# Ten chunks of a two-stage layer keep their rows in stored order, with additions moved to GpSimd and copies to other queues

## The chip, the cores and the metric

The kernel runs on one core of a Trainium2 chip. A core has engines that run side by side: TensorE (PE; its weight loads are shown as PEld), VectorE (DVE), ScalarE (ACT), GpSimd (POOL) and SyncE (SP), and 16 DMA engines that they share. The metric is the device time of one execution in microseconds; the median of several runs is given.

## The reference

Two layers follow each other. The first is a linear attention with a feature map of exponentials over 8 batches, 8 heads, 576 tokens and 64 channels; its output, put together over the heads, is `x` with shape (8, 576, 512). The second mixes `x` over the tokens in the frequency domain, with a 512 by 512 complex matrix for each of 64 modes, and closes with a channel product:

```python
X = np.fft.rfft(x, axis=1)
Y = np.zeros_like(X)
Xr, Xi = (np.real(X[:, :n_modes]), np.imag(X[:, :n_modes]))
Yr = np.einsum('bmd,mde->bme', Xr, w_r) - np.einsum('bmd,mde->bme', Xi, w_i)
Yi = np.einsum('bmd,mde->bme', Xr, w_i) + np.einsum('bmd,mde->bme', Xi, w_r)
Y[:, :n_modes] = Yr + 1j * Yi
y = np.fft.irfft(Y, n=S, axis=1)
u = x + y
return (u + np.maximum(u @ w_ch, 0.0)).astype(np.float32)
```

The mode weights `w_r` and `w_i` are 64 x 512 x 512 each and are most of what is read.

## The kernel before

The first 298 us work through 16 units of attention (four channel groups `g` by four batch pairs `bp`). They leave `x` in SBUF as bf16 (`xs`) and its spectrum (`XT`). Meanwhile the mode weights come in by loads of 1024 KB on GpSimd's DMA queue (`wload`, `next_w`); each goes to a slot of the pool `pw` (tag `wt`, eight slots). `mix` multiplies one load with the spectrum; when it has finished, the next load may take the slot.

From 298 us on, work on `x` is placed between the mixes. `x` is cut into 36 chunks `(bp, n)` of 128 rows and 512 columns, nine for each batch pair. Three stages follow.

- **Hold** (`hold`, class `Channels`). A chunk is transposed by TensorE, VectorE copies the transpose to `xT`, TensorE multiplies it with the channel weights `wchb`, and ScalarE copies the product to `xw`. The last three chunks keep their product in PSUM.
- **Absorb** (class `Absorb`). The modes are done in eight groups `o` of eight. When the first six groups are mixed, their inverse transform is added to each chunk: TensorE multiplies the table `CI` (96 rows) with `yall` (sums of the modes) and `zall` (the sums times the channel weights). VectorE adds the first to `xs`, and ScalarE writes the second, summed with the old `xw`, back to `xw`.
- **Last** (class `Last`, and the loop over `seq` at the end). When the last two groups are mixed, each pair of chunks is closed. In `base`, TensorE multiplies `xw` (result `q`) and `xs` (result `p`) with the permutation `perm`, which brings rows into stored order; the chunks of n = 8 use the identity, as their rows are in order already. In `late` it adds the last two groups through the table `CL` and the copies in `yl`. ScalarE takes the Relu of `q` into the tile `rl`, VectorE adds `p` and `rl` into an output tile `of` (slots of `pw`, tag `wt`; two of the eight hold `yall` and `yl`), and SyncE starts the store.

`put` spreads the sums: for `o` below 6 one DMA writes 16 rows of `yall` or `zall`; for `o` of 6 and 7 the sums are copied to two places each in `yl`, so that products of a pair can use different rows of TensorE at one time.

The order within each engine is the order written in the program (`InOrder` keeps it). The list `todo` holds the steps of hold and absorb, and `fill` runs some after each mix; how many is worked out from `A`, the number of steps left for the last seven mixes. `bank` gives one of four PSUM banks, `banks` one of two double banks. In `seq`, the Relu side of a pair is made one step ahead of its closing addition.

Of the kernel before, what the change touches and what calls it, by code (L numbers as in the profile page):

```python
# [19 lines left out]
DMODEL = 512  # L20
# [23 lines left out]
def kernel(  # L44
# [533 lines left out]
    CI = pb.tile([128, 5, 128], BF16, name="CI", bufs=1)  # L578
    CL = pb.tile([128, 5, 128], BF16, name="CL", bufs=1)
    perm = CF.rearrange("p c t x m -> p (c t x m)")[:, 512:640]  # L580
# [5 lines left out]
    def inverse_tables():  # L586
# [37 lines left out]
        for dst, m, r, only in ((CI, mode, r, None), (CL, late, r, None), (CM, last, rm, b0)):  # L624
            n = 512 if only is not None else 640
# [13 lines left out]
            dve.tensor_tensor(out=ang[:, :n], in0=ang[:, :n], in1=rnd[:, :n], op=ALU.add)  # L639
            yield  # L640
            act.activation(rnd[:, :n], ang[:, :n], ACT.Sin, scale=2.0 * math.pi / S_)
            if dst is CI:
                dve.tensor_scalar_mul(out=dst.rearrange("p c s -> p (c s)"), in0=rnd[:, :n],
                                      scalar1=amp)
                yield
                continue
# [5 lines left out]
            if dst is CL:  # L652
                dve.tensor_scalar_mul(out=dst[:, 4, :], in0=rnd[:, 512:640], scalar1=amp)
            yield

    class Channels:
# [4 lines left out]
        def turn(self):  # L661
            x = chunk(self.bp, self.n)
            pt = bank([128, 4, 128], BF16)
            for g in range(NG):
                pe.transpose(pt[:, g, :], x[:, g, :], ident_b)
            self.xT = pb.tile([128, 4, 128], BF16, name="xT")
            dve.tensor_copy(self.xT, pt)

# [11 lines left out]

    def back(p, c, bp, table, src, r, stop=True):

        if c < 8:
            pe.matmul(p, lhsT=table[r, c % 4, :], rhs=src[r, 2 * bp + c // 4, :],
                      start=(src is yall), stop=stop)
        else:
            for i in range(2):
                pe.matmul(p[64 * i:64 * i + 64, :], lhsT=table[r, 4, 0:64],
                          rhs=src[r, 2 * bp + i, :], start=(src is yall), stop=True)

    class Absorb:

        def __init__(self, bp, n):
            self.bp, self.n = bp, n

        def sum_p(self, p):
            self.p = p
            back(p, self.n, self.bp, CI, yall, slice(0, 96))

        def sum_q(self, q):  # L700
            self.q = q
            pe.matmul(q, lhsT=ident_b, rhs=xw[:, self.bp, self.n, :], start=True, stop=False)
            back(q, self.n, self.bp, CI, zall, slice(0, 96))

# [12 lines left out]
        def only_w(self):  # L717
            back(self.q, self.n, self.bp, CI, zall, slice(0, 96))
            self.keep_w()
# [11 lines left out]

    chunks = [(bp, n) for bp in range(NP) for n in range(9)]
    ch = [Channels(*c) for c in chunks]
    ab = [Absorb(*c) for c in chunks]
# [4 lines left out]
    def hold(i):  # L739
# [3 lines left out]
        if i < K:  # L743
            ch[i].product()
            return
        if i == K:
# [6 lines left out]
    todo = [ch[0].turn] + [lambda i=i: hold(i) for i in range(len(ch))]  # L753
    todo += [c.only_x for c in ab[K:]] + [c.only_w for c in ab[K:]] + [c.all for c in ab[:K]]
    A = 3 * 3 + K

# [5 lines left out]
    def put(src, o, dst, copies):  # L762
        if o < 6:
            sp.dma_start(dst[16 * o:16 * o + 16], src)
        else:
            for s in copies:
                r = 32 * s + 16 * (o - 6)
                (sp, pool)[s // 2 if o == 7 else 0].dma_start(yl[r:r + 16], src)


    class Last:

        def __init__(self, *items):
# [24 lines left out]
        def late(self, which):  # L798
            for a, (bp, n) in enumerate(self.items):
                r = 64 * a + 32 * which  # L800
                back((self.q if which else self.p)[a], n, bp, CL, yl,
                     slice(r, r + 16 if self.early else r + 32), not self.early)

# [10 lines left out]
        def relu(self):  # L814
            self.rl = pb.tile([128, 2, DMODEL], F32, name="rl")
            for a in range(len(self.items)):
                act.activation(self.rl[:, a], self.q[a], ACT.Relu)

        def store(self):
# [10 lines left out]
            else:  # L830
                dve.tensor_tensor(out=o, in0=self.pp, in1=self.rl, op=ALU.add)
            if n == 8:
                sp.dma_start(
# [9 lines left out]
    pairs = [[((bp, n), (bp, n + 1)) for n in (0, 2, 4, 6)] for bp in range(NP)]  # L843
    seq = [Last((0, 0)), Last((0, 1))] + [Last(*x) for x in pairs[0][1:] + pairs[1]]
    seq += [Last((0, 8), (1, 8))] + [Last(*x) for x in pairs[2]] + [Last((2, 8), (3, 8))]
    seq += [Last(*x) for x in pairs[3][:3]] + [Last((3, 6)), Last((3, 7))]
    H = DMODEL // 2
    while mixq:
# [113 lines left out]
```

## Time and profile before

| | us |
|---|---|
| median of 7 runs | 445.13 |
| lowest and highest | 443.82, 445.69 |
| the profiled execution's own time | 444.2 |
| span of the profiled execution | 442.3 |
| PE busy | 341.1 |
| DVE busy | 284.6 |
| ACT busy | 279.2 |
| POOL busy | 84.5 |

The profile is of one execution. Its span leaves out what lies around the program's instructions. A line of a timeline has the start in us from the span's start, the duration, the engine, the line, the operation with its tiles, and in brackets the idle time before it with what ended that. All instructions pass through the helper on line 37, so they are told apart by their tiles. DMA share is the mean busy share of the 16 DMA engines; a share above 1 comes from transfers that overlap in an engine.

### The profile page before, as it was taken

What the parts mean: (1) busy time and instruction counts of PE and PEld (TensorE: products, weight loads), DVE (VectorE), ACT (ScalarE), POOL (GpSimd) and SP (SyncE); (2) the same over time, 40 slices, a digit from 0 to 9 for tenths busy, and PEclk for the clock granted to TensorE, in tenths of its full rate; (3) what the DMA queues carried; (4) which work ended last, traced back from release to release, by engine and by line L of the source; (5) the groups of instructions that cost most, each with busy time, mean ns of one, the idle gap of its engine ahead of it and who ended that gap; (6) DMA issues with size and microseconds to landing.
All of it is one profiled execution on the core that took longest, in us unless ns stands there. A gap on an engine that the chain in (4) does not pass through costs nothing.

```text
span 442.3 us, 10508 instructions
## 1 busy us (share of the span) xinstructions
PE 341.1 (77%) x4433; PEld 216.4 (49%) x4433; DVE 284.6 (64%) x561; ACT 279.2 (63%) x488; POOL 84.5 (19%) x126
## 2 busy tenths in 40 slices
PE   3567768777697786795886777876899859999994
PEld 2346547645575564564754655652455424343231
DVE  4667586555756766867668668759844323876685
ACT  4598687666867976966777659433444322665673
POOL 7132122121211312321222011141011110000000
PEclk9689888688978989988888889698899999999998
DMA  8999999999999999999999999999999999993697
GB/s 170 236 211 210 238 212 237 237 212 264 210 212 237 238 236 235 213 239 210 239 220 229 234 215 240 211 213 212 211 224 221 219 219 219 212 221 80 216 382 286
DMA packets 51487, 99.31 MB, mean 225 GB/s; under 512 B 2480, under 2 KB 13616, under 8 KB 51440
## 3 DMA queue, kind: packets, MB, share of 16 engines
q0 software_dynamic: 45280, 86.19, 99.2%
q1 hardware_dynamic: 6160, 12.45, 8.1%
q8 instruction: 34, 0.56, 0.5%
q14 instruction: 13, 0.11, 0.1%
HBM read 163.64 MB, written 9.44 MB: 391 GB/s over the span
## 4 chain that ended last, share of the span: by engine, by line
issue 32%; PE 26%; DMA 14%; ACT 11%; DVE 8%; POOL 8%; POOLq 0%; ACTq 0%; DVEq 0%
DMA wt<-in_moe_w_i_dram 13%; PE pt L37 8%; PE one L37 7%; PE pp L37 5%; PE two L37 5%; POOL wt L37 4%; ACT AB L37 4%; DVE m L37 3%; ACT AQ L37 2%; DVE mk L37 2%; DVE xs L37 1%; ACT XT L37 1%; POOL qb L37 1%; ACT qT L37 1%; POOL kb L37 1%
## 5 line engine op out<-in xcount | busy, mean ns | idle before, releaser
L37 ACT ACTIVATE AB<-two 128x1024 bf16<-128x1024 f32 x64 | 62.2, 1032 | 11.6 <-DVE mk L37 8.2
L37 ACT ACTIVATE AQ<-two 128x1024 bf16<-128x1024 f32 x64 | 62.8, 1049 | 3.6 <-PE two L37 3.4
L37 ACT CAST xw<-pt 128x512 bf16<-128x512 f32 x50 | 29.4, 587 | 41.1 <-PE pt L37 41.1
L37 DVE TENSOR_REDUCE mk<-two 128x8 f32<-128x1024 f32 x32 | 38.9, 1219 | 14.5 <-PE two L37 14.5
L37 DVE TENSOR_REDUCE m<-two 128x8 f32<-128x1024 f32 x32 | 39.2, 1225 | 12.5 <-PE two L37 12.4
L37 DVE RECIPROCAL rd<-one 128x6 f32<-128x6 f32 x48 | 9.4, 196 | 54.8 <-PE one L37 54.7
L37 DVE TENSOR_TENSOR va<-vn,ee 128x1152 bf16<-128x1152 f32 x32 | 42.0, 1356 | 0.0
L37 PE MATMUL pt<-wchb,xT 128*128 128x512 bf16 x136 | 37.6, 402 | 5.6 <-DVE xT L37 4.2
L37 ACT COPY kT<-one 128x512 bf16<-128x512 bf16 (+1 forms) x32 | 19.3, 640 | 30.2 <-PE one L37 30.1
L37 PEld LDWEIGHTS <-xs 128*128 128x128 bf16 x624 | 31.8, 103 | 12.8 <-issue 7.0
L37 PEld LDWEIGHTS <-minus 96*128 96x128 bf16 x288 | 28.1, 116 | 18.5 <-issue 13.3
L37 PE MATMUL two<-w2blk,qT 128*128 128x256 bf16 x128 | 20.5, 285 | 20.7 <-ACT AB L37 10.9
L37 POOL DMA_DIRECT2D wt<-in_moe_w_r_dram x30 | 22.4, 745 | 69.4 <-PE one L37 34.8
L37 POOL DMA_DIRECT2D wt<-in_moe_w_i_dram x28 | 20.9, 746 | 75.4 <-PE one L37 42.0
L37 PE MATMUL two<-qT,w2blk 128*128 128x512 bf16 x64 | 30.3, 474 | 4.4 <-ACT AQ L37 4.1
L37 PEld LDWEIGHTS <-qT 128*128 128x128 bf16 x144 | 13.9, 99 | 37.9 <-issue 35.6
L37 PE MATMUL one<-wt,XT 128*32 128x512 bf16 x304 | 27.1, 443 | 6.6 <-DVE XT L37 2.7
L37 PE MATMUL two<-mT,minus 96*128 96x128 bf16 x256 | 30.8, 255 | 0.0
L37 PE MATMUL one<-kvz,AQ 128*128 128x65 bf16 x512 | 29.6, 217 | 0.0
L37 PEld LDWEIGHTS <-XT 128*32 128x32 bf16 x512 | 14.4, 149 | 28.1 <-issue 15.8
L37 DVE TENSOR_TENSOR xs<-one,rd 128x384 bf16<-128x384 f32 x48 | 26.8, 558 | 1.7
L37 PEld LDWEIGHTS <-AQ 128*128 128x128 bf16 x512 | 26.5, 116 | 1.4 <-issue 0.4
(131 smaller groups left out, 692.0 us busy)
## 6 DMA issues: line engine op xcount, KB each, us to landing
wt<-in_moe_w_r_dram POOLq DMA_DIRECT2D x30, 1024.0 KB, 22.1
wt<-in_moe_w_i_dram POOLq DMA_DIRECT2D x28, 1024.0 KB, 22.4
vn<-in_v_dram POOLq DMA_DIRECT2D x15, 576.0 KB, 17.6
out_dram<-of SPq DMA_DIRECT2D x16, 512.0 KB, 3.0
kb<-in_k_dram POOLq DMA_DIRECT2D x16, 288.0 KB, 15.8
qb<-in_q_dram POOLq DMA_DIRECT2D x16, 288.0 KB, 16.2
xs<-in_moe_w_i_dram POOLq DMA_DIRECT2D x2, 1024.0 KB, 24.6
yacc<-in_moe_w_r_dram POOLq DMA_DIRECT2D x1, 1024.0 KB, 9.8
```

What stands on the lines that cost most here:

```text
L37: ins = f(*args, **kwargs)
```

## The change

- Ten chunks (five pairs, the list `stored`) are turned to stored order in the hold stage: the copy to `xT` interleaves the columns, and `back_x` transposes `xT` back and writes it over the chunk in `xs`. Their absorb uses a new table `CD`, which is `CI` with interleaved columns.
- In the last stage these pairs need no `perm`; `xw` is multiplied with the identity, `xs` is not multiplied at all. GpSimd adds the chunk to the Relu result, in a tile `rx` from the slots of `pw`, and VectorE adds the late part to that.
- The four chunks of n = 8 go to the front of the list and get no absorb. In the last stage they take all eight groups at once, through `CI` with 128 rows from `yall` and `zall`, which `put` now fills for `o` of 6 and 7 too (on GpSimd's queue). Their `xs` is added by GpSimd as well.
- For `o` = 6 the copies to the upper two places of `yl` move from SyncE's queue to GpSimd's; for `o` = 7 all copies to `yl` are on SyncE's.
- The closing loop has a new order. A table `ahead` says for which pair the Relu side is made at each step; pairs whose sums go through GpSimd are made two to three steps ahead. The two double chunks of n = 8 are in a table `whole`.

```diff
+    CD = pb.tile([128, 4, 128], BF16, name="CD", bufs=1)
+    stored = [(1, 0), (1, 1), (1, 4), (1, 5), (2, 0), (2, 1), (2, 6), (2, 7), (3, 4), (3, 5)]
...
+                for a in range(2):
+                    dve.tensor_copy(
+                        CD.rearrange("k c (p a) -> k a c p", a=2)[:, a],
+                        CI[:, 0:4].rearrange("k c (a p) -> k a c p", a=2)[:, a])
...
-            dve.tensor_copy(self.xT, pt)
+            if (self.bp, self.n) in stored:
+                dve.tensor_copy(self.xT.rearrange("p g (k a) -> p g a k", a=2),
+                                pt.rearrange("p g (a k) -> p g a k", a=2))
+            else:
+                dve.tensor_copy(self.xT, pt)
+
+        def back_x(self):
+            px = bank([128, 4, 128], BF16)
+            for g in range(NG):
+                pe.transpose(px[:, g, :], self.xT[:, g, :], ident_b)
+            act.copy(chunk(self.bp, self.n), px)
...
+            self.table = CD if (bp, n) in stored else CI
...
+    chunks.sort(key=lambda c: (c[1] < 8, c not in stored))
...
             ch[i].product()
+            if chunks[i] in stored:
+                ch[i].back_x()
...
-    todo += [c.only_x for c in ab[K:]] + [c.only_w for c in ab[K:]] + [c.all for c in ab[:K]]
-    A = 3 * 3 + K
+    todo += [c.only_x for c in ab[K:]] + [c.only_w for c in ab[K:]] + [c.all for c in ab[NP:K]]
+    A = 3 * 3 + K - NP
...
-        else:
-            for s in copies:
-                r = 32 * s + 16 * (o - 6)
-                (sp, pool)[s // 2 if o == 7 else 0].dma_start(yl[r:r + 16], src)
+            return
+        for s in copies:
+            r = 32 * s + 16 * (o - 6)
+            (pool if o == 6 and s > 1 else sp).dma_start(yl[r:r + 16], src)
+        pool.dma_start(dst[16 * o:16 * o + 16], src)
...
+            self.direct = n == 8
+            self.later = self.direct or items[0] in stored
...
-                turned = perm if n < 8 else ident_b
+                turned = ident_b if self.later else perm
+                if self.later and not which:
+                    continue
...
+                if self.direct:
+                    back((self.q if which else self.p)[a], n, bp, CI, zall if which else yall,
+                         slice(0, 128))
+                    continue
...
-            self.rl = pb.tile([128, 2, DMODEL], F32, name="rl")
+            if self.later:
+                self.rl = pw.tile([128, 2, DMODEL], F32, name="rx", tag="wt")
+            else:
+                self.rl = pb.tile([128, 2, DMODEL], F32, name="rl")
             for a in range(len(self.items)):
                 act.activation(self.rl[:, a], self.q[a], ACT.Relu)
+            if self.later:
+                for a, c in enumerate(self.items):
+                    x = self.rl[:, a].rearrange("p (g e) -> p g e", g=4)
+                    pool.tensor_tensor(out=x, in0=x, in1=chunk(*c), op=ALU.add)
...
+    whole = {10: Last((0, 8), (1, 8)), 13: Last((2, 8), (3, 8))}
...
+    ahead = {1: 2, 2: 3, 3: 4, 4: 7, 5: 6, 6: 9, 7: 8, 8: 10, 9: 12, 10: 11, 11: 13, 12: 15, 13: 14,
+             14: 16, 15: 17}
     for g, s in enumerate(seq):
-        t = seq[g + 1] if 0 < g < len(seq) - 1 else None
-        if t and g > 1:
+        t = seq[ahead[g]] if g in ahead else None
+        if t and g not in (1, 3):
             t.base(1)
-        if g > 1:
+        if g > 1 and g != 3:
             s.base(0)
-            if g == 2:
-                s.late(0)
-                s.straight(0)
+        if g == 2:
+            s.late(0)
+            s.straight(0)
+            seq[4].base(1)
+            seq[3].base(0)
...
         s.store()
+        extra = [whole[g + 3]] if g + 3 in whole else [seq[5]] if g == 3 else []
+        for d in extra:
+            d.base(1)
+            d.late(1)
+            d.relu()
+        if g in whole:
+            d = whole[g]
+            d.base(0)
+            d.late(0)
+            d.store()
```

The stored pairs stand at places 5, 7, 9, 12 and 15 of the new `seq`; places 16 and 17 are single chunks.

More of the change, by code (lines that the diff above doesn't have):

```diff
@@ L578 @@
     CI = pb.tile([128, 5, 128], BF16, name="CI", bufs=1)
-    CL = pb.tile([128, 5, 128], BF16, name="CL", bufs=1)
+    CL = pb.tile([128, 4, 128], BF16, name="CL", bufs=1)
+    CD = pb.tile([128, 4, 128], BF16, name="CD", bufs=1)
+    stored = [(1, 0), (1, 1), (1, 4), (1, 5), (2, 0), (2, 1), (2, 6), (2, 7), (3, 4), (3, 5)]
     perm = CF.rearrange("p c t x m -> p (c t x m)")[:, 512:640]
@@ L624, in inverse_tables @@
         for dst, m, r, only in ((CI, mode, r, None), (CL, late, r, None), (CM, last, rm, b0)):
-            n = 512 if only is not None else 640
+            n = 640 if dst is CI else 512
             ph = calc(r, -S_ / 4.0, S_ / 4.0)
@@ L645, in inverse_tables @@
                 yield
+                for a in range(2):
+                    dve.tensor_copy(
+                        CD.rearrange("k c (p a) -> k a c p", a=2)[:, a],
+                        CI[:, 0:4].rearrange("k c (a p) -> k a c p", a=2)[:, a])
+                yield
                 continue
@@ L651, in inverse_tables @@
                     scalar1=amp)
-            if dst is CL:
-                dve.tensor_scalar_mul(out=dst[:, 4, :], in0=rnd[:, 512:640], scalar1=amp)
             yield
@@ L679, in hold, with back @@
                           start=(g == 0), stop=False)
-    def back(p, c, bp, table, src, r, stop=True):
+    def back(p, c, bp, table, src, r, stop=True, start=False):
         if c < 8:
             pe.matmul(p, lhsT=table[r, c % 4, :], rhs=src[r, 2 * bp + c // 4, :],
-                      start=(src is yall), stop=stop)
+                      start=start or src is yall, stop=stop)
         else:
@@ L694, in __init__ @@
             self.bp, self.n = bp, n
+            self.table = CD if (bp, n) in stored else CI
         def sum_p(self, p):
             self.p = p
-            back(p, self.n, self.bp, CI, yall, slice(0, 96))
+            back(p, self.n, self.bp, self.table, yall, slice(0, 96))
         def sum_q(self, q):
@@ L702, in sum_q @@
             pe.matmul(q, lhsT=ident_b, rhs=xw[:, self.bp, self.n, :], start=True, stop=False)
-            back(q, self.n, self.bp, CI, zall, slice(0, 96))
+            back(q, self.n, self.bp, self.table, zall, slice(0, 96))
         def keep_x(self):
@@ L717, in only_w @@
         def only_w(self):
-            back(self.q, self.n, self.bp, CI, zall, slice(0, 96))
+            back(self.q, self.n, self.bp, self.table, zall, slice(0, 96))
             self.keep_w()
@@ L799, in late @@
             for a, (bp, n) in enumerate(self.items):
+                if self.direct:
+                    back((self.q if which else self.p)[a], n, bp, CI, zall if which else yall,
+                         slice(0, 128))
+                    continue
                 r = 64 * a + 32 * which
                 back((self.q if which else self.p)[a], n, bp, CL, yl,
-                     slice(r, r + 16 if self.early else r + 32), not self.early)
+                     slice(r, r + 16 if self.early else r + 32), not self.early,
+                     self.later and not which)
         def straight(self, which):
@@ L831, in store @@
                 dve.tensor_tensor(out=o, in0=self.pp, in1=self.rl, op=ALU.add)
-            if n == 8:
+            if self.direct:
                 sp.dma_start(
@@ L843 @@
     pairs = [[((bp, n), (bp, n + 1)) for n in (0, 2, 4, 6)] for bp in range(NP)]
-    seq = [Last((0, 0)), Last((0, 1))] + [Last(*x) for x in pairs[0][1:] + pairs[1]]
-    seq += [Last((0, 8), (1, 8))] + [Last(*x) for x in pairs[2]] + [Last((2, 8), (3, 8))]
+    seq = [Last((0, 0)), Last((0, 1))] + [Last(*x) for x in pairs[0][1:] + pairs[1] + pairs[2]]
     seq += [Last(*x) for x in pairs[3][:3]] + [Last((3, 6)), Last((3, 7))]
+    whole = {10: Last((0, 8), (1, 8)), 13: Last((2, 8), (3, 8))}
     H = DMODEL // 2
```

## The prediction

> **What bounds the kernel now.** I read the busy shares by slice first, then the windows by stage, the timeline of the last 75 us engine by engine, and the answers for single weight loads.
>
> From the page's slices (tenths of 40 slices of 11 us):
> ```profile
> span 442.3 us, 10508 instructions
> ...
> PEclk9689888688978989988888889698899999999998
> DMA  8999999999999999999999999999999999993697
> ```
> The DMA engines are full until slice 36 (398 us), nearly idle for one slice, and busy again with the output. So there is a loading part set by DMA, and a closing part after the last weights.
>
> Windows by stage (us, then busy time of PE, PEld, DVE, ACT, POOL, then clock, DMA share, GB/s):
> ```profile
> 395.00:400.00 5.00, 5.00 (x29) 1.83 (x28) 3.88 (x8) 3.22 (x6) 0.00 (x0) 1.00 1.14 192
> 400.00:405.00 5.00, 4.85 (x27) 1.67 (x24) 3.90 (x7) 3.39 (x7) 0.00 (x0) 1.00 0.37 70
> 405.00:410.00 5.00, 4.99 (x34) 2.14 (x33) 1.83 (x5) 1.74 (x4) 0.90 (x2) 1.00 0.21 52
> 420.00:425.00 5.00, 5.00 (x34) 1.62 (x31) 4.05 (x5) 3.55 (x8) 0.00 (x0) 1.00 0.95 386
> ```
> Before 405 us PE looks full (absorbs), and DMA tapers off: one of two limits, PE or the last load. The granted clock is 1.00 throughout. GpSimd is idle.
>
> The load that the last mix needs (its issue and landing):
> ```profile
> L37 POOL DMA_DIRECT2D wt<-in_moe_w_i_dram x1: 740/740/740, 369.4 to 369.4; - x1
> ...
> DMA to landing us min/median/max: 35.7/35.7/35.7
> ```
> It lands at 369.4 + 35.7 = 405.1; the last mix starts at 405.42. PE and DMA arrive together, so freeing PE alone gains 0.3 us there.
>
> VectorE in the closing part (start, duration, and in brackets the idle time before and its releaser):
> ```profile
> 412.71 1.23 DVE L37 TENSOR_TENSOR of<-pp,rl 128x1024 f32<-128x1024 f32 x1 [1.32 <-PE pp L37]
> 415.22 6.39 DVE L37 TENSOR_TENSOR of<-pp,rl 128x1024 f32<-128x1024 f32 x5 [1.28 <-PE pp L37]
> 421.94 1.23 DVE L37 TENSOR_TENSOR of<-pp,rl 128x1024 f32<-128x1024 f32 x1 [0.34 <-PE pp L37]
> 423.58 5.17 DVE L37 TENSOR_TENSOR of<-pp,rl 128x1024 f32<-128x1024 f32 x4 [0.41 <-PE pp L37]
> 429.09 1.23 DVE L37 TENSOR_TENSOR of<-pp,rl 128x1024 f32<-128x1024 f32 x1 [0.34 <-PE pp L37]
> 430.73 5.01 DVE L37 TENSOR_TENSOR of<-pp,rl 128x1024 f32<-128x1024 f32 x4 [0.41 <-PE pp L37]
> 435.66 0.68 DVE L37 TENSOR_TENSOR ofr<-pp,rl 128x512 f32<-128x512 f32 x1
> 436.58 0.69 DVE L37 TENSOR_TENSOR ofr<-pp,rl 128x512 f32<-128x512 f32 x1 [0.24 <-ACT rl L37]
> ```
> VectorE makes a pair of output rows every 6.39 / 5 = 1.28 us. A PE step takes 1.30 us (its base multiplications for successive pairs start at 424.70 and 426.00). So from 415.22 to 437.27 two engines are level, and VectorE idles only 2 x (0.34 + 0.41) = 1.50 us, at the two pairs of n = 8. The stores run at 386 GB/s with DMA share 0.95: a third limit close by.
>
> **The sum's frame.** The profiled execution took 444.2 us: 442.3 of span and 1.9 around it. The median of the seven runs is 445.13, 0.93 higher; I work on 444.2 and add 0.93 at the end. About 0.2% (0.9 us) is what a measurement of this kernel can tell from no change.
>
> **Holding stage, 298 to 372 us: cost nothing.** Ten chunks get four transposes back (0.23 us of PE each: a transpose group starts at 328.40, the next group at 328.63), a ScalarE copy (0.64, the kT copy's row) and a strided xT copy (0.42 now; a strided 128x128 copy took 0.30, so 0.7 for 512). That is 2.3 us of PE, 6.4 of ACT, 2.8 of DVE, and under 1 us for CD's two copies. What hides it is PE's idle time before weights land: 1.74 at 350.20, 0.91 at 355.53, 3.23 at 361.69, 5.9 us in all. Without that cover it would cost about 2.6 us. Weight issues come a little later, but each load now queues 32 to 38 us.
>
> **Absorb stage, 372 to 405 us.** Four n = 8 absorbs go. Three are whole, 0.99 us of PE each (390.61 to 391.60). The fourth goes in two parts of 0.33; another chunk takes its place among the last three, 0.65 becoming 0.44. Together 3.86 us, so PE could be at the last mix at 405.42 - 3.86 = 401.6, or 402.9 with the waits for earlier loads (about 1.3). An idle time of about 1 us does not slow PE: after 0.91 idle at 355.53 four products took 1.03 us, while after 3.23 idle at 361.69 eight small ones took 1.89 against 1.04.
>
> So the landing decides. The loads of 351.17, 356.50, 362.67 and 369.40 land after 35.8, 37.6, 37.4 and 35.7: at 387.0, 394.1, 400.1, 405.1. Undisturbed spacing is 5.0 (the load of 346.49 lands after 35.5, at 382.0), so three loads took 18.1 instead of 15.0. In that stretch SyncE's queue carries the four copies of the o = 6 sums (4 x 128 KB, issued 385.91 to 389). The change leaves two there; the other two, and the two new writes into yall and zall, go on GpSimd's queue, in program order behind all weight loads (last issue 369.40). Half of 3.1 is **1.55 us earlier**. Bounds: at the 220 GB/s of these windows 256 KB take 1.2; at most 2.4, where PE itself arrives (402.9 with 0.1 to start). The later landing of the two copies is free: pair (0,2) needs them at 409.97, some 5 us after the weights.
>
> At o = 7 both copies of each sum go on SyncE, one after the other (0.55 an issue), where GpSimd's copy was issued at 409.66 and PE waited for it until 413.36. Same time within 0.3 us. Behind them on SyncE is only the first store (410.37).
>
> **Closing stage, in the times of before.**
> - Removed: ten base multiplications of x (5 x 0.44 us of PE), the four n = 8 ones, and the 1.50 us of VectorE idle time that follows the n = 8 groups. VectorE still adds every pair, 15 x 1.28 + 1.5.
> - Moved: two pairs of base multiplications go ahead of the wait for yl. But pair 3's two Relus then start at 413.9 and last 1.08, so VectorE starts on it at 415.1 against 415.22. Nothing gained.
> - Added: 14 GpSimd adds of 128x512 between Relu and VectorE. No such row exists. The same add on VectorE takes 0.69; GpSimd's one-input 128x128 row took 0.292 and an empty MEMSET 0.098, so 512 elements take 0.098 + 4 x 0.194 = 0.87 with one input and up to 0.098 + 8 x 0.194 = 1.65 with two. I take **1.1**, between these; both ends stay for the range.
>
> Three more waits follow. ScalarE makes Relus in the order 3, 4, 5, 7, 6: from 413.9 five pairs at 1.09, so pair 6 is ready at 419.4. Pair 5's first half is ready at 416.7; two adds end at 418.95, and VectorE, due at 417.66, starts pair 5 at 419.0 and pair 6 at 420.3. Twelve pairs at 1.28 from there and 1.5 for the two single rows end at 437.1, against 437.27: the idle time that goes is spent at pair 5. Later adds fit while 14 of them from 416.75 end before pair 15 is due at 434.4, that is up to 1.26 each.
>
> Last, buffers. The early Relu results (rx) take the same six free slots as the output tiles. An output tile holds one 1.23 + 3.0 us (landing of a store), 3.3 slots at this pace; seven rx of about 5 us in 16 us hold 2.2. Of six slots 5.5 are full, so jitter becomes stalls; with PSUM waits at the two extra pairs I take **0.6**, between 0 and 1.6 (stores that land at 3.4, the top of the usual rows, at each reuse). Tail: -0.2 + 0.6 = **+0.4**.
>
> The Trainium skill's GPSIMD Engine Reference, section "Elementwise — side-by-side cycle accounting", speaks against this step: it gives 4497 ns for a 2048-element fp32 add on GpSimd and 2293 on VectorE. A quarter of that is an estimate of 1.12 us and a fixed part, and with 1.2 the sum would be 0.2 us later than mine. Its SBUF page ("SBUF — State Buffer", "Who interferes with whom") has VectorE and GpSimd lock a shared port pair; by its rule a VectorE add with one input in PSUM would not wait, and nothing in this trace shows either.
>
> **Sum.** 444.2 - 1.55 + 0.4 = 443.05, 1.15 less; on the median 445.13 - 1.15, **444.0 us**. Own range of this case 443.0 to 445.0.
>
> **The rivals.**
> - GpSimd becomes the bound. It decides from 1.26 us an add. At 1.4 the 14 adds end at 436.35 and the tail at 439.1, +1.9; at 1.65 at 439.85 and 442.6, +5.3. With -1.55 the kernel ends at 445.5 to 448.9. For it: two inputs, one strided and of another type. Against: it needs the upper third of my price. Chance 0.25.
> - The queue change brings nothing, because the last load is late for another reason (the taper from 400 to 405 us), or the copies only move: -0 + 0.4, 445.5. Against it: the spacing of 5.0 before 387 and 7.1 right after. Chance 0.15.
> - Both terms at their better ends: last mix when PE is ready (-2.4), adds at 0.87 or less and no slot stalls (ScalarE's order then sets pair 6 at 419.45, the tail is 1.0 shorter): 441.7. Chance 0.15.
> - My forecast: 0.45.
>
> **Chances and range.** Faster by over 0.2% (below 444.24): 0.30 of my forecast's 0.45 and the 0.15 of the better ends, 0.45. Within 0.2%: 0.15 of the forecast, 0.05 of the queue rival, 0.03 of the first, 0.23. Slower: 0.10 and 0.22, 0.32. The range 441.7 to 447.5 leaves out GpSimd's price above 1.55 (about 0.1) and gains beyond both better ends.
>
> **What would show it.** Last landing at 403.5 and last mix within 0.3 of it, PE idle about 1 us before; a GpSimd row of 14 adds at 1.1 us; VectorE idle about 1.3 us before pair 5, then pairs at 1.28 with waits on store landings. It is wrong if the adds take over 1.26 us, if the landing stays at 405, or if PE still loses time in the holding stage.

## The result: 0.4% slower, and the profile after

The changed kernel takes 446.47 us (median of 15 runs, 445.47 to 447.70) against 444.73 for the kernel before beside it (36 runs): a ratio of the means of 1.0042, 95% interval 1.0032 to 1.0051. A second set of four runs gave 447.57 and 1.0067 [1.0046, 1.0088]. The forecast was 444.0, with faster as the likeliest sign; the sign was wrong. That the time still lies inside the outer range of 441.7 to 447.5 is luck: the upper part of that range was there for GpSimd as the bound, and GpSimd was not the bound. The profiled execution took 446.47 us, 2.27 more than the one before; its span is 444.4 us, where it was 442.3.

The windows by stage (us, then busy time of PE, PEld, DVE, ACT, POOL, then clock, DMA share, GB/s):

```profile
400.00:405.00 5.00, 3.72 (x21) 1.40 (x19) 1.98 (x3) 1.66 (x3) 0.00 (x0) 1.00 0.58 100
405.00:410.00 5.00, 5.00 (x27) 2.28 (x21) 1.47 (x4) 1.33 (x3) 0.53 (x1) 0.66 0.56 85
410.00:415.00 5.00, 4.47 (x21) 1.39 (x19) 2.61 (x3) 2.18 (x4) 0.53 (x1) 1.00 0.84 165
420.00:425.00 5.00, 5.00 (x33) 1.35 (x32) 4.19 (x4) 4.41 (x9) 5.00 (x6) 1.00 0.75 307
```

PE is no longer full from 400 to 405 us. In the next window it is full again, but the granted clock is 0.66 where it was 1.00. DMA is busier from 405 to 415 (0.56 and 0.84, before 0.21 and 0.63) and less busy from 420 (307 GB/s, before 386).

The load of the last mix (duration and issue, and its time to landing), and PE's timeline around it:

```profile
L37 POOL DMA_DIRECT2D wt<-in_moe_w_i_dram x1: 740/740/740, 367.5 to 367.5; - x1
...
DMA to landing us min/median/max: 37.1/37.1/37.1
```

```profile
399.28 0.67 PE L37 MATMUL pt<-wt,XT 128*32 128x512 bf16 x8 [1.04 <-DMA wt<-in_moe_w_r_dram]
404.62 0.66 PE L37 MATMUL pt<-wt,XT 128*32 128x512 bf16 x8 [1.13 <-DMA wt<-in_moe_w_i_dram]
407.18 1.92 PE L37 MATMUL pt<-wchb,yT 128*128 128x256 bf16 x8
415.17 0.39 PE L37 MATMUL pt<-yl,CL 32*128 32x512 bf16 x2 [0.70 <-DMA yl<-zst]
```

The last load lands at 367.5 + 37.1 = 404.6, before at 405.1. PE waits 1.04 and 1.13 us for the last two loads; before it waited for neither. Then eight products take 1.92 us; the same eight took 1.04 before. They make `zst`, the last sums times the channel weights, from which the last copies into `yl` are taken. The timeline of before at the same place:

```profile
405.42 0.66 PE L37 MATMUL pt<-wt,XT 128*32 128x512 bf16 x8
...
407.50 1.04 PE L37 MATMUL pt<-wchb,yT 128*128 128x256 bf16 x8
...
408.63 0.42 DVE L37 CAST zst<-pt 128x256 bf16<-128x256 f32 x1 [1.07 <-PE pt L37]
```

VectorE from the last sums on (start, duration, idle before it and releaser):

```profile
409.19 0.42 DVE L37 CAST zst<-pt 128x256 bf16<-128x256 f32 x1 [2.32 <-PE pt L37]
...
413.38 1.22 DVE L37 TENSOR_TENSOR of<-pp,rl 128x1024 f32<-128x1024 f32 x1 [1.31 <-PE pp L37]
416.20 1.23 DVE L37 TENSOR_TENSOR of<-pp,rl 128x1024 f32<-128x1024 f32 x1 [1.60 <-ACT rl L37]
418.50 1.23 DVE L37 TENSOR_TENSOR of<-pp,rl 128x1024 f32<-128x1024 f32 x1 [1.07 <-PE pp L37]
420.08 1.23 DVE L37 TENSOR_TENSOR of<-pp,rx 128x1024 f32<-128x1024 f32 x1 [0.36 <-POOL rx L37]
421.22 1.21 DVE L37 TENSOR_TENSOR of<-pp,rl 128x1024 f32<-128x1024 f32 x1
422.36 1.21 DVE L37 TENSOR_TENSOR of<-pp,rx 128x1024 f32<-128x1024 f32 x1
424.30 1.23 DVE L37 TENSOR_TENSOR of<-pp,rl 128x1024 f32<-128x1024 f32 x1 [0.73 <-PE pp L37]
425.74 1.22 DVE L37 TENSOR_TENSOR of<-pp,rx 128x1024 f32<-128x1024 f32 x1 [0.22 <-POOL rx L37]
...
428.67 1.23 DVE L37 TENSOR_TENSOR of<-pp,rx 128x1024 f32<-128x1024 f32 x1 [0.42 <-DMA out_dram<-of]
...
438.38 0.69 DVE L37 TENSOR_TENSOR ofr<-pp,rl 128x512 f32<-128x512 f32 x1 [0.24 <-issue]
```

From these rows, with those of before, the 2.1 us of span are laid out from mark to mark (us):

| from, to | before | after | difference |
|---|---|---|---|
| start of the last mix | 405.42 | 404.62 | -0.80 |
| to VectorE's half of `zst` | 3.21 | 4.57 | +1.36 |
| to the addition of pair 2 | 4.08 | 4.19 | +0.11 |
| to the addition of pair 3 | 2.51 | 2.82 | +0.31 |
| to VectorE's end | 22.05 | 22.87 | +0.82 |
| to the end of the span (stores) | 5.03 | 5.33 | +0.30 |

So 0.80 is gained and 2.90 lost. The first loss stands beside the clock, that of VectorE's end beside waits for PE, GpSimd and slots. A second profile of each kernel, taken later, repeats the losses one by one (1.36, 0.12, 0.28, 0.83 and 0.39, together 2.98), but not the gain: there the last mix starts 2.04 sooner (404.69 for 406.73). GpSimd's group row (busy, mean ns):

```profile
L37 POOL TENSOR_TENSOR rx<-rx,xs 128x512 f32<-128x512 f32 x14 | 15.7, 1158 | 7.1 <-issue 7.1
```

GpSimd is busy without a break from 417.78 to 433.44, but VectorE waits for it only before pairs 5 and 9 (0.36 and 0.22).

### The profile page after: what moved, and what is told of

It reads as the page before. It is cut to its first block, busy times and chain, and to the rows that moved or that the text cites. A ratio compares the mean times of both kernels' runs of the same rounds, so it can differ in the third digit from the quotient of the medians.

```text
span 444.4 us, 10558 instructions
## 1 busy us (share of the span) xinstructions
PE 336.9 (76%) x4439; PEld 218.2 (49%) x4439; DVE 284.6 (64%) x558; ACT 281.7 (63%) x494; POOL 102.3 (23%) x144
## 4 chain that ended last, share of the span: by engine, by line
issue 27%; DMA 21%; PE 20%; DVE 13%; ACT 10%; POOL 7%; POOLq 0%; SPq 0%; DVEq 0%; ACTq 0%
DMA wt<-in_moe_w_i_dram 12%; PE one L37 8%; DMA wt<-in_moe_w_r_dram 7%; PE pt L37 6%; PE two L37 5%; ACT AB L37 4%; POOL wt L37 4%; DVE m L37 3%; DVE mk L37 2%; ACT AQ L37 2%; DVE of L37 2%; DVE xw L37 2%; PE pp L37 1%; ACT XT L37 1%; DMA yl<-zst 1%
## 5 line engine op out<-in xcount | busy, mean ns | idle before, releaser
L37 ACT CAST xw<-pt 128x512 bf16<-128x512 f32 x48 | 28.2, 587 | 36.9 <-PE pt L37 36.9
L37 PE MATMUL pt<-wchb,xT 128*128 128x512 bf16 x136 | 34.9, 379 | 7.4 <-DVE xT L37 4.6
L37 POOL DMA_DIRECT2D kb<-in_k_dram x16 | 11.5, 718 | 80.9 <-PE one L37 80.1
```

The costliest lines, as they stand in the source:

```text
L37: ins = f(*args, **kwargs)
```

## The experiments

Theory A: PE, with less absorb work, waits for the last weights, and the granted clock halves behind that. Theory C: the new writes into `yall` and `zall` at `o` = 7 hold up the copies into `yl`. Rivals: B (less PE work is harmless), G (GpSimd's additions), P (the order of the closing loop), S (the stores are the limit). In the expectations D stands for PE's order in the closing loop, Q for a queue change worth 0.45 us, V for a last landing that varies and decides, and B, in the run with two tiles to a slot, for buffers. Ratios are to the kernel before on the same chip, with 95% intervals.

### PE kept busy before the last two mixes

```diff
+        if len(mixq) < 2:
+            idle = bank()
+            for j in range(5):
+                pe.matmul(idle, lhsT=ident_b, rhs=wchb[:, j % 4, :], start=True, stop=True)
         mix(*key, wts.pop(key), XTb[g % 2], bank)
```

> The changed kernel with five extra products of 512 columns (0.22 us each, into a scratch bank that nobody reads) on TensorE before each of the last two mixes, where it waits 1.04 and 1.13 us for weights. Theory A (the clock): the waits let the granted clock fall to half for 3.4 us, right in the chain from the last mix to zst; with TensorE kept busy the clock stays at 1.00 in 405 to 410 us, the eight products of wchb and yT take 1.04 us and not 1.92, the closing adds start 1.3 to 1.6 us earlier, and the kernel takes about 445.0, level with the one before. Rival B (the chain is late for another reason, its DMA copies or VectorE): the clock may stay up, but the time moves by less than 0.4 us, 446.1 to 446.6.

448.22 us, 1.0071 [1.0051, 1.0090]. PE's timeline and two windows:

```profile
406.63 1.04 PE L37 MATMUL pt<-wchb,yT 128*128 128x256 bf16 x8
414.53 0.37 PE L37 MATMUL pt<-yl,CL 32*128 32x512 bf16 x1 [1.91 <-DMA yl<-zst]
```

```profile
405.00:410.00 5.00, 5.00 (x32) 2.20 (x28) 2.33 (x6) 2.08 (x5) 1.06 (x2) 1.00 0.60 90
...
415.00:420.00 5.00, 4.73 (x17) 0.88 (x16) 1.23 (x1) 3.19 (x6) 1.46 (x2) 0.50 0.48 195
```

The clock stays at 1.00 here, the eight products take 1.04 again and `zst` is ready 1.43 us sooner: that half of A holds. But the copies into `yl` now land 6.3 us after their issue (median), PE waits 1.91 us for them, and the clock drops there, in the closing part, where pair 4 waits 2.56 us. The wait and the loss have moved, and the kernel is no faster than the changed one (1.0042 and 1.0067): A's time of 445.0 is missed.

### Less PE work in the kernel before

```diff
-    todo += [c.only_x for c in ab[K:]] + [c.only_w for c in ab[K:]] + [c.all for c in ab[:K]]
-    A = 3 * 3 + K
+    todo += [c.only_x for c in ab[K:]] + [c.only_w for c in ab[K:]] + [c.all for c in ab[:K] if c.n < 8]
+    A = 3 * 3 + K - 3
```

> The kernel before, with the three whole absorbs of n = 8 left out (those rows lack the first 48 modes); nothing else is changed. It takes 2.97 us from TensorE ahead of the last mix and adds nothing. Theory A: TensorE then waits for the last weights (landing 405.1), the clock falls after the last mix, and the kernel is slower than before by 0.8 to 1.5 us, 445.6 to 446.3, with a granted clock under 0.8 in 405 to 410 us. Rival B: work taken away cannot cost; the same or up to 0.3 us faster, 444.4 to 444.8, clock 1.00.

444.72 us, 0.9994 [0.9983, 1.0005]. The last mix starts at 405.91; the waits stand earlier, at 351.92 and 363.42 (2.44 and 3.38), and the clock from 405 on is 1.00. So less PE work alone neither gains nor harms: B's number, and a miss for A's. But PE didn't wait for the last weights here, as A's condition asks (the load lands at 405.5). From the mix at 369.97 to the last one are 35.94 us, 1.06 less than in the kernel before, and the rest of the 2.97 left out shows as short waits for VectorE and ScalarE. So this run says nothing on what such a wait does to the clock.

### The queues of the copies as before

```diff
-            (pool if o == 6 and s > 1 else sp).dma_start(yl[r:r + 16], src)
+            (sp, pool)[s // 2 if o == 7 else 0].dma_start(yl[r:r + 16], src)
```

> The changed kernel with the copies into yl on the queues they had before: all four of o = 6 on SyncE, the upper ones of o = 7 on GpSimd; the new writes into yall and zall stay on GpSimd. The prediction's step: two copies fewer beside the weights bring the last load 1.55 us forward, so here it lands 1 to 1.5 us later than 404.6, and the kernel is 1 us or more slower, 447.5. Rival: the landing was late by one laggard DMA engine and hardly depends on it (404.6 to 405.1, as the changed kernel gained only 0.5); and the copies of o = 7 land 0.5 to 1 us earlier, as SyncE has one fewer to issue ahead; then 446.0 to 446.6.

446.98 us, 1.0046 [1.0027, 1.0064]. The last landing is at 405.0, 0.5 later than after. PE waits 0.78 before the last mix and the clock stays at 1.00, but the copies into `yl` land 5.4 us after issue (median) and PE waits 1.41 us for them. They are late with either queue, so the queue isn't what delays them.

### No additions on GpSimd

```diff
-            if self.later:
-                for a, c in enumerate(self.items):
-                    x = self.rl[:, a].rearrange("p (g e) -> p g e", g=4)
-                    pool.tensor_tensor(out=x, in0=x, in1=chunk(*c), op=ALU.add)
```

> The changed kernel without the 14 GpSimd adds (x is missing from the rows of the stored pairs and of n = 8). If GpSimd's adds hold up the closing part (the rival of the prediction), it ends 1.5 us or more earlier, 445.0 or less. If TensorE's order does (pair 4's closing products are queued behind the Relu products of pairs 5 and 7, which wait for PSUM banks that ScalarE frees), only the 0.36 us before pair 5 and 0.22 before pair 9 go, and the kernel takes 445.9 to 446.5, with the idle time of 1.07 us before pair 4 still there.

447.28 us, 1.0056 [1.0037, 1.0074]; x is missing in those rows. PE's waits at pairs 4 and 8 (1.07, 1.03) stay. In this profile the wait before the last mix is 2.23 and the clock 0.50, so the times don't compare; but from pair 3 to VectorE's end it takes 23.03 us without the additions, and 22.87 with them. GpSimd is not the cause of the loss.

### The o = 7 writes after the store of pair 3

```diff
-        pool.dma_start(dst[16 * o:16 * o + 16], src)
+        if o == 7:
+            put_late.append((dst, src))
+        else:
+            pool.dma_start(dst[16 * o:16 * o + 16], src)
...
         s.store()
+        if g == 3:
+            for dst, src in put_late:
+                sp.dma_start(dst[112:128], src)
```

> The changed kernel with only the two o = 7 writes into yall and zall moved: SyncE issues them after the store of pair 3, some 6 us later; the double chunks of n = 8 read them after that. Theory C (the new writes hold up the copies into yl, which go to partitions beside theirs at the same time): the copies of the last sums land 3.4 to 3.8 us after their issue and not 4.3 to 4.8 (6.2 to 6.4 in the run with TensorE kept busy), pair 3 starts 0.6 to 1 us earlier, 445.4 to 445.9. Rival: the copies are slow because SyncE issues both, or because of the stores behind them; then the landing stays above 4.2 and the time at 446.5.

448.69 us, 1.0073 [1.0046, 1.0100]. The copies into `yl` land after 3.3 to 3.6 us, as before the change: C's landing holds. The clock is 0.90 from 400 and 0.50 from 405 us, after a wait of 1.12, and the time is no better. The next run tells whether that is the reason.

### Both mends together

The edits of the first and the last run in one kernel.

> The same with five extra products before each of the last two mixes. Theories A and C together: the clock stays at 1.00 and the yl copies land 3.4 to 3.8 us after their issue at 408.3 to 408.9, so pair 3 starts by 414.0 (416.20 in the changed kernel, 416.51 with TensorE kept busy alone); closing part as before from there: 444.0 to 444.6. If C is wrong, TensorE waits for yl as in the run with TensorE kept busy, and the time is 447 to 448.

445.79 us, 1.0017 [1.0005, 1.0029], 2.9 us less than the run above, from which it differs by the scratch products alone. The clock is 1.00 up to 435 us and pair 3 starts at 414.23, 1.97 sooner than after. The span is only 0.7 shorter than after, since the closing part grows from 22.87 to 24.0 us; by the ratios (1.0042 and 1.0067, to 1.0017) 1.1 to 2.2 us of the loss come back. The copies into `yl` land after 3.8 to 5.3 us, where the first run with scratch products had 5.3 to 7.1: the two writes are worth 1.1 us of the median without these products and 1.8 with them, but something else still delays some of the copies here, and no run shows what. Part of the closing part's growth my own late writes made; PE's weight loads wait for them:

```profile
421.10 0.14 PEld L37 LDWEIGHTS <-CI 128*64 128x64 bf16 x4 [1.28 <-DMA zall<-zst]
```

### The order of pairs 4 and 8

```diff
-        if g > 1 and g != 3:
+        if g > 1 and g not in (3, 4, 8):
             s.base(0)
...
-        if g > 2:
+        if g > 2 and g not in (4, 8):
             s.late(0)
...
+        if g in (3, 7):
+            seq[g + 1].base(0)
+            seq[g + 1].late(0)
```

On top of both mends, and alone on the kernel after:

> The same again, with the closing products (p) of pairs 4 and 8 issued on TensorE before the extra Relu products (q) of pair 5 and of the double chunk, not after. Theory D (TensorE's order): the idle times of VectorE before pairs 4 and 8 (1.07 and 0.73 us, PE pp) go, 1 to 1.5 us less than the run without it, 442.8 to 443.4, if the stores keep up. Rival: ScalarE's Relus or the stores set the pace, and it moves under 0.4 us.

> The changed kernel with the order of f3's products alone. Theory D: 1 to 1.5 us faster, 445.0 to 445.5, with no wait of VectorE for TensorE over 0.4 us after pair 3. Rival as above: 446.1 to 446.6.

445.81 us, 1.0022 [1.0007, 1.0036], and 448.49, 1.0081 [1.0063, 1.0099]. PE's wait at pair 4 goes, but pair 5 then waits 1.54 us for GpSimd (1.98 alone), and three additions wait 2.5 us in all for stores to free slots. One wait takes the place of another.

### Two tiles to a slot

```diff
+    def half():
+        if not halves:
+            t = pw.tile([128, 2, 2, DMODEL], F32, name="oh", tag="wt")
+            halves.extend([t[:, 0], t[:, 1]])
+        return halves.pop(0)
...
-                self.rl = pw.tile([128, 2, DMODEL], F32, name="rx", tag="wt")
+                self.rl = half()
```

The output tile `of` in the same way; the second kernel also leaves GpSimd's additions out.

> The same as the run with the late and position part of pairs 4 and 8 first, but each 8 KB slot of the pool now serves two output tiles or Relu results of 4 KB, so 12 are free instead of 6. Theory S (the stores are the limit): a pair is 524 KB, at the 390 GB/s of the windows 1.34 us, so a VectorE that does not wait for slots only runs ahead of the stores. VectorE's waits for landings (0.67, 1.26 and 0.54 us in that run) go, its last addition ends 1.5 to 2.5 us earlier (some 22 us after pair 3 starts), but the last stores land 5 us and more after their issue instead of 3.4, and the time stays at 445.2 to 445.8. Theory B (buffers): the stores have room, and the time falls by the waits, to 443.3 to 444.3. Theory G (GpSimd): its adds come too late for pairs 5 and 9 whatever the slots, the waits become waits for GpSimd of over 1 us each, time 445 to 446.

> The run with two tiles to a slot, and without GpSimd's 14 additions in the closing part: x is missing in those rows, so the time tells only what the adds and their order cost. Theory G: VectorE's waits for GpSimd (1.5 us at pair 5) go and the time falls by about that, to 443.5 to 444.3. Theory S: pair 5 starts earlier, the stores queue up more, and the time stays within 0.4 us of the run with the adds.

445.62 us, 1.0024 [1.0006, 1.0042], and 444.94, 0.9998 [0.9987, 1.0010]. The waits for slots are gone and nothing is gained by it: the stores now land 4.3 us after issue (median; 4.0 with the order alone, 3.1 in the kernel before). The second is 0.7 us quicker (the intervals just overlap), so GpSimd's turn at pair 5 costs up to that, as G said, once the rest is mended. Without the additions DMA is full from 420 on:

```profile
425.00:430.00 5.00, 5.00 (x36) 1.51 (x32) 4.20 (x4) 4.01 (x9) 0.00 (x0) 1.00 1.01 408
430.00:435.00 5.00, 4.19 (x26) 1.25 (x23) 4.98 (x5) 3.10 (x6) 0.00 (x0) 1.00 0.98 386
435.00:440.00 5.00, 1.60 (x4) 0.29 (x3) 2.84 (x4) 0.60 (x1) 0.00 (x0) 0.69 1.01 395
```

At 395 GB/s the 524 KB of a pair take 1.33 us, as long as PE's step of 1.30 before the change. VectorE had ended at 438.3, and the span at 443.8. That is S, a limit close under the kernel before.

### The n = 8 part alone, and the writes one pair sooner

```diff
-    stored = [(1, 0), (1, 1), (1, 4), (1, 5), (2, 0), (2, 1), (2, 6), (2, 7), (3, 4), (3, 5)]
+    stored = []
...
+    ahead = {g: g + 1 for g in range(1, 17)}
...
-        extra = [whole[g + 3]] if g + 3 in whole else [seq[5]] if g == 3 else []
+        extra = [whole[g + 3]] if g + 3 in whole else []
```

With both mends; the later three have `if g == 2` for the late writes, the second of them keeps the stored pairs, the third also has the order and the slots of above.

> One part of the change alone: no chunk is stored in order ahead of time, only the four n = 8 chunks skip the absorb stage and go through GpSimd; the closing order is again one pair ahead. The two late writes and the products that keep TensorE busy before the last two mixes are kept. Theory P (the closing loss comes from the five pairs that run two to three steps ahead): pairs follow at 1.28 to 1.30 us as before, without the 1.07 and 1.6 us waits for PE, pair 3 starts at about 414.2 and VectorE ends some 22 us later, time 443.5 to 444.6, under the kernel before. Theory S: with the two extra writes among the stores the end comes no earlier than 0.6 us under that of the run with the stored pairs, 445 to 445.8. If the n = 8 chunks cause the loss: waits at the two double chunks, 445.5 to 446.5.

> The n = 8 part alone again, with the two writes into yall and zall issued one pair sooner, after the store of pair 2 instead of pair 3 (in the run before, TensorE stood 2.27 us for the landing of zall and VectorE 3.00). Theory P (the five stored pairs make the closing loss, the n = 8 part alone gains): the wait for zall goes, VectorE ends 2 to 3 us sooner, the time falls from 445.9 to 443.0 to 444.3, below the kernel before. Theory S (512 KB a pair at 390 GB/s is the limit): the end moves by less than 1 us, 445.0 to 445.6, and the stores of the last ten pairs land 4 us and more after their issue instead of 3.5.

> The run with late writes and TensorE kept busy, writes one pair sooner as above; the stored pairs and GpSimd's additions stay. The wait of 1.28 us for zall ahead of pair 8 goes. Theory P: the waits at pairs 4 and 5 (1.07 and 0.37 us) stay, time 444.6 to 445.4, some 1 us above the n = 8 part alone. Theory S: as slow as the n = 8 part alone, both 445.0 to 445.8.

> All mends together: TensorE kept busy, late writes one pair sooner, position parts of pairs 4 and 8 first, two tiles to a slot. Theory P/G: VectorE's waits shrink to GpSimd's at pair 5 (1.5 us), pair 8 no longer waits 1.65 for PE, end 1 us earlier than with the later writes, 444.3 to 445.0. Theory S: VectorE ends earlier, stores land 5 us after issue, time within 0.4 us of the 445.6 of that run.

The first gave 445.94 us, 1.0031 [1.0016, 1.0046], with 2.27 us of waiting for `zall` as my writes came too late. With the writes sooner: 444.45, 0.9989 [0.9973, 1.0006] for the n = 8 part; 445.12, 0.9996 [0.9980, 1.0013] with the stored pairs; 445.77, 1.0006 [0.9991, 1.0022] with all mends. VectorE in the n = 8 part alone, then with the stored pairs:

```profile
415.33 6.43 DVE L37 TENSOR_TENSOR of<-pp,rl 128x1024 f32<-128x1024 f32 x5 [1.02 <-ACT rl L37]
422.99 3.82 DVE L37 TENSOR_TENSOR of<-pp,rl 128x1024 f32<-128x1024 f32 x3 [1.23 <-PE pp L37]
...
436.54 0.69 DVE L37 TENSOR_TENSOR ofr<-pp,rl 128x512 f32<-128x512 f32 x1 [0.24 <-ACT rl L37]
```

```profile
413.50 1.23 DVE L37 TENSOR_TENSOR of<-pp,rl 128x1024 f32<-128x1024 f32 x1 [1.01 <-ACT rl L37]
415.80 1.22 DVE L37 TENSOR_TENSOR of<-pp,rl 128x1024 f32<-128x1024 f32 x1 [1.07 <-PE pp L37]
...
436.02 0.69 DVE L37 TENSOR_TENSOR ofr<-pp,rl 128x512 f32<-128x512 f32 x1 [0.24 <-issue]
```

The closing part takes 437.23 - 415.33 = 21.90 us with the n = 8 part alone and 436.71 - 413.50 = 23.21 with the stored pairs: by these profiles the five pairs made ahead cost 1.3 us and save nothing there. Against the kernel before (22.05) the n = 8 part saves 0.15: the four short waits at the n = 8 pairs (1.50) go, as the prediction said, but a wait of 1.23 for PE, which makes a double chunk's Relu side first, and two of 0.2 take their place. It also meets the stores: its DMA share from 415 to 440 is 0.93 to 1.02. The two medians differ by 0.7 us with intervals that overlap, so for the times this is an indication only. With the stored pairs, the scratch products and the sooner writes the loss of the change is gone (0.9996), and nothing is gained.

### The queue part alone, and both kernels once more

```diff
-                (sp, pool)[s // 2 if o == 7 else 0].dma_start(yl[r:r + 16], src)
+                (sp, pool)[s // 2].dma_start(yl[r:r + 16], src)
```

on the kernel before, twice; then the kernels before and after unchanged.

> The kernel before with one part of the change alone: the two upper copies of the o = 6 sums into yl go on GpSimd's queue. My step said 1.55 us of landing. Theory Q (0.45 us, as the run with the old queues showed): last landing 404.5 to 404.7, and since TensorE has absorbs until 405.4 the gain is 0 to 0.5: 444.6 to 445.1. If 1.55 holds, the landing is 403.6 and TensorE still limits to about 0.3 us of gain, so it is the landing that tells them apart.

> The kernel before with the queue part alone, once more. If its gain is real, 443.4 to 444.2 and a ratio of 0.995 to 0.998 again; if the first result was chance, 444.4 to 445.2. Theory V: last landing at 404.6 or sooner, and the last mix within 0.2 us of 405.4, where TensorE is ready.

> The kernel before once more, for a second profile of it. The queue part alone gained 1.4 us in the times and 0.4 us in the one profile, and the profiled execution of before was 0.93 us under its median. Theory V (the last landing varies between executions, and in most of before's the weights come later than TensorE): this profile has the last landing after 405.4, TensorE waits for it, and an own time of 444.8 to 445.6. If the landing is again 405.1 or less with TensorE the later of the two at an own time near 445, the gain of the queue part lies somewhere else.

> The kernel after once more, for a second profile. Theory A (TensorE waits of 1 us and more halve its clock): the clock of 405 to 410 us is under 0.8 if the wait before the last mix is 1.0 us or more, and 1.00 if it is under 0.85, as in the other profiles. Theory C: copies of the o = 7 sums land 4.3 us and later. Time 446.1 to 447.1.

The queue part alone: 443.74 us, 0.9967 [0.9951, 0.9982], and 444.08, 0.9987 [0.9975, 1.0000]. It is the only version that has an interval wholly under 1, though its second one touches 1. Before: 444.96, 0.9999 [0.9986, 1.0013]. PE in that second profile of before:

```profile
351.71 0.66 PE L37 MATMUL pt<-wt,XT 128*32 128x512 bf16 x8 [2.52 <-DMA wt<-in_moe_w_i_dram]
...
363.12 0.66 PE L37 MATMUL pt<-wt,XT 128*32 128x512 bf16 x8 [3.31 <-DMA wt<-in_moe_w_i_dram]
369.73 0.66 PE L37 MATMUL pt<-wt,XT 128*32 128x512 bf16 x8
...
406.73 0.65 PE L37 MATMUL pt<-wt,XT 128*32 128x512 bf16 x5
```

The last mix is 1.31 later than in the first profile (405.42), though its load landed at 405.1 again. From the mix at 369.73 to the last are 37.00 us, and 37.00 in the first profile too (368.42 to 405.42), and 36.98 and 36.99 with the queue part. So theory V (the last landing varies and decides) falls: from 363 us on PE sets the pace of the kernel before, and what varies between executions is when the weights near 350 to 363 us land. With the queue part the last mixes start at 405.48 and 405.43, so its gain isn't there. In the profiles 0.4 us of it lies at the very end: from VectorE's last addition to the end of the span are 4.6 us in both, and 5.0 in both profiles of before, while the last store lands 3.6 to 3.7 us after that addition in all four. SyncE closes the kernel with eight waits on semaphores, one after another and about 0.06 us apart. In the kernel before the last landing (440.93) releases the first of them; with two copies fewer on SyncE (440.96) it releases the seventh. From that landing to the end are 1.34 us in the one and 0.97 in the other. No row shows the rest, and it stays open; the second set, with 0.6 us in all, leaves little of it.

The second profile of after has the wait before the last mix (1.85), clock 0.66, and `zst` 4.57 us after the mix begins, as the first.

## Why the prediction was wrong, point by point

**Right.** The holding stage costs nothing: the last load is issued at 367.49, 1.91 sooner than before (370.01 for 370.70 in the second profiles). PE idles about 1 us before the last mix (1.13, then 1.85). A GpSimd addition costs 1.1 us (15.66 / 14 = 1.12) and is not the bound; VectorE's additions last 1.21 to 1.23 us beside GpSimd's as well as without them. That pair 5 waits for GpSimd is right too, but the 1.3 foretold shows only where PE doesn't hold up pair 4 first (1.54 with the new order); in the changed kernel a wait of 1.07 for PE at pair 4 hides most of it, and 0.36 is left.

On the span the sum foretold -1.55 + 0.4 = -1.15 and +2.10 came, 3.25 more. Four steps make that up: 1.47 from the clock, 0.75 from the start of the last mix, 0.31 from the copies into `yl` ahead of pair 3, 0.72 from the tail. The clock's 1.47 are the 1.36 to `zst` and the 0.11 to pair 2; with PE kept busy both go (3.21 and 4.09 us, as before).

**Wrong, and the largest term, put at nothing: "An idle time of about 1 us does not slow PE".** I had taken it from one wait of 0.91. After the wait of 1.13 PE ran at half its clock for 3.4 us (405.88 to 409.29), and the way from the last mix to `zst` took 1.36 more. Scratch products before the mix bring the clock to 1.00 and those 1.43 us back, and between the two runs with late writes, where the slow clock had lasted 6.8 us, they alone make 2.9 us: that shows the cause. Alone it doesn't turn the sign: without the 1.47 the sum of the first profiles is still +0.63, and the run with the scratch products alone was no faster. Only with the writes moved as well is the loss gone (1.0017, and 0.9996 with the writes sooner). The Trainium skill's "TensorE: Matmul & The Clock Gate", Part 1, has the clock follow PE's activity in free-running windows of 3413 ns; the loss here is as long as one window, though the waits of 1.04 and 1.13 are much shorter than the idle gaps of over 3 us that its table of rules warns of.

**Wrong in size: the 1.55 us of the queue change.** The last landing is 0.5 sooner (404.58 for 405.08), and 0.4 in the second profiles (404.65 for 405.06). Over 16 profiles with the new queue for `o` = 6 it lies between 403.2 and 406.3, mean 404.7; over four with the old at 405.0 to 405.5. The step gave the two moved copies half of a delay of 3.1 us, read from one profile in which three loads took 18.1 us; in the second profile of the same kernel they took 16.7, with the queue part alone 17.2 and 16.6, and 16.3 in both profiles of the changed kernel. The times of the queue part alone say 0.6 and 1.5 us (ratios 0.9987 and 0.9967), of which 0.4 have nothing to do with the weights. And "PE and DMA arrive together" was one execution's chance: in the kernel before PE sets the last mix, 0.34 and 1.67 us after the landing. That its start moved by 0.80 and 2.04, on both sides of the 1.55, is luck for this term: 0.34 and 1.67 of it are PE's lateness, which the step didn't count.

**Not costed: the two new writes at o = 7.** I priced the copies' queues ("same time within 0.3 us") but not the 256 KB that run beside them. Landings grew from 3.5 to 4.6 us (median; 3.3 to 6.0), and without the two writes they are back at 3.3 to 3.6. In after only 0.3 of it shows, since the slow clock makes all else late too; with the clock mended it was a wait of 1.91.

**Wrong in size: the tail, +0.4.** It was +0.82 at VectorE and +0.30 in the stores behind. The term "with PSUM waits at the two extra pairs I take **0.6**" is the one: those waits alone are 1.07 and 0.73. It also rested on VectorE at 1.28 us a pair, from 6.39 / 5. The five start (6.39 - 1.23) / 4 = 1.29 apart, which is PE's step of 1.30. Without waits VectorE starts pairs 1.14 apart (421.22, 422.36), so it was not level with PE, and the stores at 1.33 are the limit just behind.

With my steps as measured the sum is -0.80 + 1.36 + 0.11 + 0.31 + 0.82 + 0.30 = +2.10 on the span.

## What to carry to other kernels

Taking work off an engine that waits for a load at the end of a stage turns work into idle time, and on TensorE the idle time can cost more than was gained (here 1.36 us against 0.80, and 2.04 in the second profiles); look at the granted clock after such a wait before counting it as free. Before calling two limits level from one profile, take a second one: the one that has the same distance between its steps in both (here PE, 37.00 us twice) is the bound. A new transfer is to be costed for what it does to the transfers that run beside it, not only for its place in a queue.

## What the runs showed of the hardware that was not expected

- The wait before the last mix against the clock from 405 to 410 us, in nine profiles: 1.12, 1.13, 1.85 and 2.23 us gave 0.50 to 0.66; 0.70, 0.78, 0.79, 0.89 and 0.94 gave 1.00 (three of these with the scratch products just ahead). But in the kernel before a wait of 1.74 at 350.20 and, once more, one of 2.52 at 351.71 left it at 1.00, and only later ones of 3.23 and 3.31 were followed by 0.50 and 0.68 (364 to 366 us). Length alone doesn't decide. Nor does PE's busy time in the 3.41 us ahead of a drop, the length that a drop has at the least: 2.28 in after and 2.32 in the run with late writes alone, but 1.97 (346.49 to 349.90) and 1.52 (347.67 to 351.08) in the two profiles of before, where the clock stayed up. What decides was not found.
- Copies from SBUF to SBUF of 128 KB took 3.3 to 3.8 us in the kernel before, with four issued within 3 us, and up to 7.1 with six. But four took 3.8 to 5.3 in the run with both mends, so the number isn't all.
- VectorE additions of 1024 elements from PSUM last 1.22 us each by their rows but start 1.14 apart.
- The stores go at 386 to 408 GB/s at a DMA share of 0.98 to 1.01 (the three windows of the run without additions). The skill's page "DMA: Bandwidth & Descriptors", "Specifications", puts a core's HBM limit at about 358; here, with one core at work, the measurement is above it.
